# Attention, a dense FFN and a routed top-1 FFN on one core: the routing's comparisons made ahead, the last pass's tiles turned together, the last item's turns in other banks

## The chip, the cores and the metric

The kernel runs on one core of one Trainium2 chip. The metric is the device time of one execution in microseconds (us); lower is better. TensorE does the matmuls and transposes, VectorE (DVE), ScalarE (ACT) and GpSimd (POOL) the elementwise work, and DMA queues issued by SyncE (SP) and GpSimd move the data.

## What is computed

```python
x = softmax(rot(q) @ rot(k).T / 8) @ v        # 2 batches, 8 heads, 576 tokens, 64 wide -> 1152 x 512
h = x @ w_in                                  # 512 -> 2048
x = (h * sigmoid(1.702 * h)) @ w_out          # 2048 -> 512
logits = x @ w_gate                           # 8 experts
e = argmax(logits); gate = softmax(logits)[e]
out[i] = gate[i] * (relu(x[i] @ w1[e]) @ w2[e])   # 512 -> 1024 -> 512
```

A token counts only if fewer than 288 tokens before it chose the same expert; otherwise its row stays zero. So each token needs its rank among the tokens of its expert. Data and weights are float32.

## The kernel before

Weights and activations are split into a high and a low half (`hl`, `gh`, `gl`), and each product is three matmuls. ScalarE makes the high half and VectorE the low one (`halves` L833 and L834; `relu` L899 and L900). The splits of the weights live in a ring of four; the raw weights come through the buffers `wf`.

Attention goes first, in eight pairs of heads. Then the dense FFN runs in three passes over the tokens, at columns `CUTS` 0, 512, 768 and 1152. `first(k0, k1)` does a pass: `ffn` (first product `h` L853, second product `y` L883), then the finished rows `row` (L927) of 128 tokens each, which go to DRAM as `x2`, and their logits. The first two passes get the logits by eight dot products of a row on VectorE (L945). The last pass does it tile after tile on TensorE: four transposes into a bank `tr` (L936), a copy `yt` (L938), four matmuls with the gate weights into `lt` (L941) and a copy to `logits` (L942).

When all logits of a batch are known, `route(b)` runs: 25 comparisons of 128 x 128 on VectorE (L974, `before`: does a token stand ahead of another in the order that counts), 25 small matmuls that turn them into ranks (`rank` L1010), many small VectorE steps, and `r_at` (L1047), the place of each token in the list of its expert. Five scatters by GpSimd (`slots` L1059) write the list. `gather` reads it back (`ent` L1131) and fetches the tokens' rows of `x2` by indirect DMA (`got` L1136). `turn` transposes these (`tg` L1154) and splits them (`xt` L1162, L1163).

The routed FFN then works on items: `STATIC = (3, 96), (2, 112), (3, 96), (1, 96)`, that is blocks and tokens of a block; items 0 and 1 are of batch 0, items 2 and 3 of batch 1. Items 0 to 2 go through `second`: weights by `slice_of`, the products by `ffn`, the result to `yt`, transposed back, scaled by the gate (`row`) and scattered to `out` (L1183, GpSimd). `turn(i + 1)` is called from a hook of item i. Item 3, 96 tokens, goes through `few`, where the tokens stand in the partitions and the inner activations are transposed in a bank `tf` (L1251) that belongs to the same pool (`ps_m`) as all other transposes. It is a generator: its first product is issued in item 2's end. Its last row is scaled in two halves, by ScalarE (L1284) and VectorE (L1285). A loop behind it, for tokens beyond the four items, isn't entered.

Each engine does its instructions in order. The order isn't written out in this part: a scheduler chooses it from the program's order, the dependences and its estimate of times, so a change in one place can move instructions in others.

Of the kernel before, what the change touches and what calls it, by code (L numbers as in the profile page):

```python
# [25 lines left out]
P = 128  # L26
# [191 lines left out]
def consts():  # L218

    half = D // 2  # L220
    inv_freq = 1.0 / 10000.0 ** (np.arange(0, half, dtype=np.float32) / half)
    freqs = np.outer(np.arange(S, dtype=np.float32), inv_freq)
    cos, sin = np.cos(freqs), np.sin(freqs)
    main, rest = places()
    place = np.concatenate([rest, main, rest, rest])
    d = np.arange(P) % D
    cs, sn = (x[place][:, d % half].T for x in (cos, sin))
    sn = np.where((d < half)[:, None], -sn, sn)
    turns = np.stack([cs, sn], axis=1)
# [12 lines left out]
    c = np.clip(np.arange(-OFF, NC * P), 0, S - 1)  # L242
    order = np.concatenate([
        np.repeat((c // HALF * HALF + col[c % HALF])[None], P, 0),
        place.reshape(P, -1),
        valid.reshape(P, -1),
        (FAR * (1 - valid)).reshape(P, -1),
    ], axis=1)
# [9 lines left out]
    return {  # L258
        "turns": turns,
        "ident": ident,  # L260
        "rows": rows,
        "pad": pad,
        "order": order.astype(np.float32),
        "small": np.repeat(small.astype(np.float32)[None], P, 0),
    }
# [452 lines left out]
class Experts:  # L718


    def __init__(self, ctx, tc, d, cst, xt, weights):
# [6 lines left out]
        self.made, self.open, self.dots = {}, {}, []  # L728
# [32 lines left out]
    def prepare(self):  # L761
# [17 lines left out]
        self.order = one.tile([P, OFF + NC * P + 3 * B * NC], F32, name="order")  # L779
# [19 lines left out]
    def setup(self):  # L799
# [6 lines left out]
        load(self.order, d["order"])  # L806
        load(self.small, d["small"])
# [51 lines left out]
    def ffn(self, x, slices, act, hook=None, rows=False):  # L859
# [8 lines left out]
        for f in range(n + LAG):  # L868
            while len(hls) < min(n, f + 2):
                hls.append(slices[len(hls)]())  # L870
            if hook and f == n - hook[0]:
                hook[1]()
# [31 lines left out]
    def first(self, k0, k1, hook=None):  # L904
# [13 lines left out]
        y = self.ffn(self.xt[:, :, :, k0:k1], slices, self.gated, hook, rows=True)  # L918
# [6 lines left out]
        for k, t in zip(range(k0 // P, k1 // P), y):  # L925
            row = self.three.tile([P, DM], F32, name="row")
            nc.scalar.activation(out=row, in_=t, func=AF.Copy)  # L927
# [4 lines left out]
            out = [self.logits[b][:, k - b * (NC - 1)] for b in range(B) if 0 <= k - b * (NC - 1) < NC]  # L932
            if last:
                t = self.ps_m.tile([P, 512], F32, tag="m", name="tr")
                for j in range(ND):
                    nc.tensor.transpose(t[:, j * P:(j + 1) * P], row[:, j * P:(j + 1) * P], self.cst["ident"])  # L936
                yt = self.two.tile([P, ND, HALF], F32, name="yt", bufs=1)[:, :, 0:P]
                nc.vector.tensor_copy(out=yt, in_=t.rearrange("p (j c) -> p j c", j=ND))  # L938
                t = self.ps_m.tile([P, 512], F32, tag="m", name="lt")[:, 0:E]
                for j in range(ND):  # L940
                    nc.tensor.matmul(t, yt[:, j], self.gate[:, j], start=j == 0, stop=j == ND - 1)  # L941
                nc.vector.tensor_copy(out=out[0], in_=t)  # L942
                continue
            for e in range(E):
                nc.vector.scalar_tensor_tensor(  # L945
# [7 lines left out]
                )  # L953
            for x in out[1:]:
                nc.vector.tensor_copy(out=x, in_=out[0])

    def route(self, b, L):
# [34 lines left out]
        at = OFF + NC * P  # L992
        place, valid, away = (self.order[:, at + (B * i + b) * NC:at + (B * i + b + 1) * NC] for i in range(3))
        sequence = self.order[:, OFF * (1 - b):OFF * (1 - b) + NC * P]
# [13 lines left out]
        for i in range(NC):  # L1008
            for k in range(NC):
                nc.tensor.matmul(  # L1010
                    rank[:, i], before[i][:, k], oh[:, k], start=k == 0, stop=k == NC - 1
                )
# [34 lines left out]
        placed = v.tensor_copy(out=at, in_=lin)  # L1047
        ls, ex, sm, gate = big("ls"), big("ex"), col("sm"), col("gate")
# [146 lines left out]
    def second(self, ent, x, expert, hook=None, ahead=None):  # L1195
# [4 lines left out]
        y = self.ffn(x, [lambda f=f: self.slice_of(expert, f) for f in range(F2 // P)], self.relu, hook)  # L1200
# [3 lines left out]
        if ahead:  # L1204
            next(ahead)
# [10 lines left out]
    def few(self, ent, x, expert):  # L1216
# [6 lines left out]
        raws, parts = [], []  # L1223
# [24 lines left out]
        def turned(g):  # L1248
            t = self.ps_m.tile([P, 2, size], F32, tag="m", name="tf")
# [11 lines left out]
        for k in range(n + 1):  # L1261
# [38 lines left out]
    def run(self):  # L1300
# [6 lines left out]

        self.logits = [self.two.tile([P, NC, E], F32, name=f"logits{b}", bufs=1) for b in range(B)]
        for n, (k0, k1) in enumerate(zip(CUTS, CUTS[1:])):
            self.first(k0, k1, {0: (10, self.setup), len(CUTS) - 2: (0, lambda: turn(0))}.get(n))  # L1310
            if n == 0:
                self.clear()
            for b in range(B):
                if k0 < (b + 1) * S <= k1:
                    self.route(b, self.logits[b])
                    for k in range(2 * b, 2 * b + 2):
                        found[k] = self.gather(k, [b], *STATIC[k])
        def few():
            yield from self.few(found[3][0], x[3], self.expert(3, sp))

        last = few()
        for i in range(3):
            hook = (4, 0, 4)[i], lambda: turn(i + 1)
            self.second(found[i][0], x[i], self.expert(i, sp), hook, last if i == 2 else None)
        for _ in last:
            pass
# [41 lines left out]
```

## Time and profile before

| | |
|---|---|
| time, median of 3 runs | 452.94 us (452.74 to 454.37) |
| the profiled execution | 453.61 us |
| its span in the trace | 451.9 us |
| mean granted TensorE clock | 0.985 of full speed |
| PE busy | 428.3 us (95%), 3190 matmuls |
| PE weight loads (PEld) | 353.2 us (78%) |
| DVE busy | 343.3 us (76%) |
| ACT busy | 265.3 us (59%) |
| POOL busy | 134.3 us (30%) |
| DMA | 59.28 MB, mean 131 GB/s |

Times in the trace count from the span's start; 1.7 us of the execution lie outside the span. A matmul's row in a timeline may stand for several in sequence (x4), and matmuls overlap, so the step from one start to the next is shorter than one's duration. In brackets stands how long the engine was idle before an instruction and what ended that.

### The profile page before, as it was taken

How to read it: one execution, taken by the hardware profiler on the slowest of the kernel's cores; microseconds unless marked ns; L12 is line 12 of the kernel's file. 1: busy time of each engine (PE TensorE's matmuls, PEld its weight loads, DVE VectorE, ACT ScalarE, POOL GpSimd, SP SyncE). 2: the span in 40 equal slices, each digit the busy share in tenths (PEclk: the TensorE clock that was granted, in tenths of full speed). 3: DMA queues.
4: the chain of work that ended last, by engine and by line, in shares of the span. 5: the costliest groups of instructions: out<-in, count | busy, mean ns of one | idle time of the engine just before them, and what ended most of it. 6: DMA issues, size and time to landing. Idle time of an engine off the chain costs nothing.

```text
span 451.9 us, 8634 instructions
## 1 busy us (share of the span) xinstructions
PE 428.3 (95%) x3190; PEld 353.2 (78%) x3190; DVE 343.3 (76%) x815; ACT 265.3 (59%) x556; POOL 134.3 (30%) x129
## 2 busy tenths in 40 slices
PE   6799999999999999999999999999999999499994
PEld 3566666666675888888899999989889999499982
DVE  5777867788988899995599988988454899255662
ACT  1688988988786234445566665744472555163562
POOL 0988769692338000000000000003350025501011
PEclk9999999999999999999999999999999999699998
DMA  8534422612351866662133001000764346936501
GB/s 271 211 114 147 147 72 77 241 30 94 97 175 70 269 197 228 216 248 93 46 135 123 3 0 48 0 2 0 280 211 140 116 131 178 261 94 217 195 20 51
DMA packets 20542, 59.28 MB, mean 131 GB/s; under 512 B 3397, under 2 KB 5637, under 8 KB 20496
## 3 DMA queue, kind: packets, MB, share of 16 engines
q1 hardware_dynamic: 17872, 54.28, 35.9%
q0 software_dynamic: 1664, 3.62, 2.8%
q10 hardware_dynamic: 960, 0.79, 0.5%
q8 instruction: 27, 0.44, 0.4%
q14 instruction: 19, 0.16, 0.1%
HBM read 52.09 MB, written 6.67 MB: 130 GB/s over the span
## 4 chain that ended last, share of the span: by engine, by line
PE 71%; issue 13%; POOL 6%; DMA 4%; DVE 3%; ACT 1%; POOLq 0%; DVEq 0%
PE y L883 24%; PE h L853 23%; PE t L607 8%; PE s L492 6%; PE t L532 6%; PE s L753 2%; PE s L481 2%; POOL qk L465 2%; POOL out L1183 2%; DMA qk<-in_qk 1%; DMA slots<-entry,r_at 1%; DMA turns<-in_turns 1%; POOL qk L467 1%; POOL slots L1059 1%; DMA ent<-slots 1%
## 5 line engine op out<-in xcount | busy, mean ns | idle before, releaser
L853 PE MATMUL h<-xt,hl 128*128 128x256 f32 (+4 forms) x828 | 148.4, 320 | 0.0
L853 PEld LDWEIGHTS h<-xt,hl 128*128 128x128 f32 x828 | 129.8, 192 | 10.3
L834 DVE TENSOR_TENSOR hl<-wf,hl 128x1024 fp32r<-128x1024 f32 x69 | 84.6, 1226 | 23.6 <-ACT hl L833 23.3
L833 ACT ACTIVATE hl<-wf 128x1024 fp32r<-128x1024 f32 x69 | 73.1, 1061 | 40.7 <-PE y L883 21.5
L883 PE MATMUL y<-hl,gh 128*128 128x512 f32 x288 | 81.0, 392 | 0.0
L1059 POOL DMA_INDIRECT slots<-entry,r_at x10 | 13.9, 1390 | 202.6 <-DVE r_ends L970 200.2
L883 PEld LDWEIGHTS y<-hl,gh 128*128 128x128 f32 x288 | 52.9, 188 | 9.2
L504 DVE TENSOR_SCALAR_CACHE_REDUCE pp<-s 128x576 f32<-128x576 f32 x64 | 45.9, 754 | 13.6 <-PE s L492 13.0
L516 ACT ACTIVATE pp<-pp,nm 128x576 f32<-128x576 f32 x64 | 49.3, 776 | 11.3 <-DVE pp L504 11.1
L893 ACT ACTIVATE g<-h 128x256 f32<-128x256 f32 (+2 forms) x45 | 21.8, 484 | 55.6 <-PE h L853 55.5
L465 POOL TENSOR_TENSOR qk<-qk,turns 128x640 f32<-128x640 f32 (+1 forms) x30 | 44.8, 1509 | 21.3 <-DMA qk<-in_qk 21.3
L883 PE MATMUL y<-hl,gl 128*128 128x512 f32 x144 | 48.2, 392 | 0.0
L492 PE MATMUL s<-qk 64*128 64x288 f32 x256 | 40.4, 421 | 2.7 <-DVE qk L467 1.9
L607 PE MATMUL t<-pt,vr 128*64 128x288 f32 x256 | 38.0, 417 | 0.0
L532 PEld LDWEIGHTS t<-ident,pp 64*128 64x128 f32 x576 | 25.8, 138 | 13.1 <-issue 4.2
L883 PE MATMUL y<-gh,hl 128*128 128x288 f32 (+1 forms) x192 | 35.4, 297 | 0.0
L945 DVE SCALAR_TENSOR_TENSOR dot<-row,dots 128x512 f32<-128x512 f32 x48 | 33.0, 687 | 1.6 <-ACT row L927 1.2
L895 DVE TENSOR_TENSOR gl<-g,gh 128x512 fp32r<-128x512 f32 (+2 forms) x48 | 26.7, 562 | 9.6 <-ACT gh L894 9.6
L413 ACT ACTIVATE pt<-t 128x512 f32<-128x512 f32 (+1 forms) x55 | 28.5, 543 | 7.8 <-PE t L532 7.6
L532 PE MATMUL t<-ident,pp 64*128 64x64 f32 x576 | 29.8, 229 | 1.6 <-ACT ptr L413 1.1
L492 PEld LDWEIGHTS s<-qk 64*128 64x128 f32 x256 | 24.1, 188 | 7.5 <-DVE qk L467 2.8
L883 PEld LDWEIGHTS y<-hl,gl 128*128 128x128 f32 x144 | 26.2, 188 | 4.2
(185 smaller groups left out, 608.4 us busy)
## 6 DMA issues: line engine op xcount, KB each, us to landing
wf<-in_w SPq DMA_DIRECT2D x32, 512.0 KB, 4.7
qk<-in_qk SPq DMA_DIRECT2D x14, 640.0 KB, 5.0
raw<-in_w_in SPq DMA_DIRECT2D x16, 512.0 KB, 4.0
raw<-in_w_out SPq DMA_DIRECT2D x16, 512.0 KB, 4.3
vr<-in_v SPq DMA_DIRECT2D x8, 320.0 KB, 3.9
out<-got SPq DMA_DIRECT2D x9, 256.0 KB, 3.1
dots<-in_w_dots SPq DMA_DIRECT2D x4, 512.0 KB, 4.1
x<-row SPq DMA_DIRECT2D x8, 256.0 KB, 2.4
```

Of the source, the lines that this page charges most:

```text
L413: return e.activation(out=out, in_=x, func=AF.Copy)
L465: e.tensor_tensor(out=u, in0=u, in1=self.turns[:, k, ts], op=ALU.mult)
L492: nc.tensor.matmul(both[h][:, n, 0:HALF], q[hs, at:at + P], k[hs, key:key + HALF], start=True, stop=True)
L504: self.nc.vector.tensor_scalar(out=self.room(p, i).rearrange("p (n k) -> p n k", n=2), in0=self.open.pop(("s", p, i))[:, :, 0:HALF], scala ...
L516: self.nc.scalar.activation(out=x, in_=x, func=AF.Exp, scale=-1.0, bias=self.nm[p % 2][:, i:i + 1], accum_out=self.sum[p % 2][:, i:i + 1],)
L532: self.nc.tensor.transpose(banks[b][:, at:at + 64], x[bs], self.ident[bs, bs])
L607: self.nc.tensor.matmul(o[h * 64:h * 64 + 64], x, y, start=j < 2, stop=j > 7)
L833: ins = nc.scalar.activation(out=hl[:, 0], in_=t, func=AF.Copy)
L834: self.last = nc.vector.tensor_tensor(out=hl[:, 1], in0=t, in1=hl[:, 0].bitcast(F32), op=ALU.subtract).ins
L853: ins = self.nc.tensor.matmul(h, u, v, start=m == 0, stop=m == len(ops) - 1)
L883: nc.tensor.matmul(y[j][:, 0:DM if rows else w], u, v, start=f == LAG and m == 0, stop=f == n + LAG - 1 and m == 2,)
L945: nc.vector.scalar_tensor_tensor(out=self.weights.m2.tile([P, DM], F32, tag="m", name="dot"), in0=row, scalar=1.0, in1=self.dots[e], op0=A ...
```

## The change

The comparisons of batch b leave `route(b)` and become `compare(b)`, called from hooks in the passes in front: batch 0's in the second pass, batch 1's in the last. There are five of 128 x 640 for a batch, instead of 25 of 128 x 128, and they are written into the two buffers that held raw weights. Their operand, `sequence`, is an input of its own now, loaded into the `yt` tile.

In the last pass `turned_logits` turns the three tiles into three banks (one of the second product, two of `ps_m`), with copies by VectorE, ScalarE and VectorE; the logits of all three go into one bank and are copied once. The three rows are copied by ScalarE, VectorE and ScalarE. `route` and `gather` are called by `known(k)` as soon as the logits of a batch's last tile are there. The dot products of the second pass that come behind `route(0)` are ordered behind its `r_at` (`placed`).

In the last item, `few` is no generator any more, the transposes `tf` use two banks of the second product (`y1`, `y2`), and the last row is scaled by one ScalarE instruction.

```diff
     def first(self, k0, k1, hooks, known):
...
-        for k, t in zip(range(k0 // P, k1 // P), y):
+        work = []
+        for n, (k, t) in enumerate(zip(range(k0 // P, k1 // P), y)):
             row = self.three.tile([P, DM], F32, name="row")
-            nc.scalar.activation(out=row, in_=t, func=AF.Copy)
+            if last and n % 2:
+                nc.vector.tensor_copy(out=row, in_=t)
+            else:
+                nc.scalar.activation(out=row, in_=t, func=AF.Copy)
...
-            if last:
-                t = self.ps_m.tile([P, 512], F32, tag="m", name="tr")
-                for j in range(ND):
-                    nc.tensor.transpose(t[:, j * P:(j + 1) * P], row[:, j * P:(j + 1) * P], self.cst["ident"])
-                yt = self.two.tile([P, ND, HALF], F32, name="yt", bufs=1)[:, :, 0:P]
-                nc.vector.tensor_copy(out=yt, in_=t.rearrange("p (j c) -> p j c", j=ND))
-                t = self.ps_m.tile([P, 512], F32, tag="m", name="lt")[:, 0:E]
-                for j in range(ND):
-                    nc.tensor.matmul(t, yt[:, j], self.gate[:, j], start=j == 0, stop=j == ND - 1)
-                nc.vector.tensor_copy(out=out[0], in_=t)
-                continue
+        if last:
+            self.turned_logits(work)
+            known(k1 // P - 1)
+            return
...
+                if self.placed:
+                    self.tc.add_manual_dep(ins.ins, self.placed, Weights.order, reason="order")
...
+    def turned_logits(self, work):
+        nc = self.nc
+        yt = self.two.tile([P, ND, HALF], F32, name="yt", bufs=1)
+        spare = lambda: self.ps_y[3].tile([P, 512], F32, tag="y3", name="tr")
+        rooms = [yt[:, :, 0:P], yt[:, :, P:2 * P], self.three.tile([P, DM], F32, name="got", bufs=4)]
+        rooms[2] = rooms[2].rearrange("p (j c) -> p j c", j=ND)
+        for n, (row, out) in enumerate(work):
+            t = self.ps_m.tile([P, 512], F32, tag="m", name="tr") if n else spare()
+            for j in range(ND):
+                nc.tensor.transpose(t[:, j * P:(j + 1) * P], row[:, j * P:(j + 1) * P], self.cst["ident"])
+            t = t.rearrange("p (j c) -> p j c", j=ND)
+            if n % 2:
+                nc.scalar.activation(out=rooms[n], in_=t, func=AF.Copy)
+            else:
+                nc.vector.tensor_copy(out=rooms[n], in_=t)
+        t = spare()[:, 0:len(work) * E].rearrange("p (n e) -> p n e", e=E)
+        for n, (row, out) in enumerate(work):
+            for j in range(ND):
+                nc.tensor.matmul(t[:, n], rooms[n][:, j], self.gate[:, j], start=j == 0, stop=j == ND - 1)
+        nc.vector.tensor_copy(out=self.logits[B - 1][:, NC - len(work):], in_=t)
+
+    def compare(self, b):
+        at = OFF * (1 - b)
+        rooms = [self.weights.room().rearrange("p a b -> p (a b)").bitcast(BF16) for i in range(2)]
+        self.before = [rooms[k // 3][:, k % 3 * NC * P:(k % 3 + 1) * NC * P] for k in range(NC)]
+        for k in range(NC):
+            place = self.order[:, b * NC + k:b * NC + k + 1]
+            self.nc.vector.tensor_scalar(
+                out=self.before[k], in0=self.sequence[:, at:at + NC * P], scalar1=place, scalar2=None, op0=ALU.is_gt
+            )
...
     def route(self, b, L):
...
-        before = []
-        for i in range(NC):
-            x = self.one.tile([P, NC, P], BF16, name="before", bufs=2)
-            for k in range(NC):
-                ts(x[:, k], sequence[:, i * P:(i + 1) * P], place[:, k:k + 1], ALU.is_gt)
-            before.append(x)
...
     def few(self, ent, x, expert):
...
-            t = self.ps_m.tile([P, 2, size], F32, tag="m", name="tf")
+            j = 1 + len(turns) % 2
+            t = self.ps_y[j].tile([P, 512], F32, tag=f"y{j}", name="tf")[:, 0:2 * size]
...
-            if k == 0:
-                yield
...
-        half = DM // 2
-        nc.scalar.activation(out=row[:, half:], in_=y[:, half:], func=AF.Copy, scale=gate)
-        nc.vector.tensor_scalar(out=row[:, 0:half], in0=y[:, 0:half], scalar1=gate, scalar2=None, op0=ALU.mult)
+        nc.scalar.activation(out=row, in_=y, func=AF.Copy, scale=gate)
...
+            hooks = {10: self.setup}, {8: lambda: self.compare(0)}, {8: lambda: self.compare(1), 0: lambda: turn(0)}
+            self.first(k0, k1, hooks[n], known)
```

**The order on VectorE, in the routing of batch 1.** `r_...` are the routing's small steps, `hl` and `gl` the splits for item 0. Before:

```order
L1005 CAST r_s_3855<-r_s_3854 128x8
L834 TENSOR_TENSOR hl_74<-wf,hl_74 128x1024
L900 SCALAR_TENSOR_TENSOR gl<-h,gh 128x288
L974 TENSOR_SCALAR before<-order 128x128 x10
L980 SCALAR_TENSOR_TENSOR r_kc<-r_left,count 128x8
L834 TENSOR_TENSOR hl_75<-wf,hl_75 128x1024
L974 TENSOR_SCALAR r_items<-r_kc 128x8
L980 SCALAR_TENSOR_TENSOR r_key<-r_kc,small 128x8
L900 SCALAR_TENSOR_TENSOR gl<-h,gh 128x288
L974 TENSOR_SCALAR before<-order 128x128 x5
L980 SCALAR_TENSOR_TENSOR r_items<-r_kc,r_items 128x8
```

With the change:

```order
L1032 CAST r_s_3802<-r_s_3801 128x8
L903 SCALAR_TENSOR_TENSOR gl<-h,gh 128x288
L837 TENSOR_TENSOR hl_74<-wf,hl_74 128x1024
L1005 TENSOR_TENSOR r_far<-rank,r_left 128x40
L1015 SCALAR_TENSOR_TENSOR r_kc<-r_left,count 128x8
L1015 SCALAR_TENSOR_TENSOR r_far<-r_far,rank 128x40
L1009 TENSOR_SCALAR r_items<-r_kc 128x8
L1015 SCALAR_TENSOR_TENSOR r_key<-r_kc,small 128x8
L1015 SCALAR_TENSOR_TENSOR r_items<-r_kc,r_items 128x8
L1005 TENSOR_TENSOR r_sq<-r_key 128x64
L1012 TENSOR_REDUCE r_ni<-r_items 128x1
L903 SCALAR_TENSOR_TENSOR gl<-h,gh 128x288
```

The comparisons are gone from here, and the ranks are read (`r_far`) right behind the first split. Counted on to `r_at`, five `gl` of item 0 stand ahead of it now, eight before.

**The order on TensorE, from the last pass's end into item 0.** `tr` are the transposes of the rows; with L979 `tr` is the bank of the logits, L941 (`lt`) before. Before:

```order
L1154 MATMUL tg<-ident,got 128x96 x4
L936 MATMUL tr<-ident,row 128x128 x4
L941 MATMUL lt<-gate,yt 128x8 x4
L853 MATMUL h<-xt,hl_74 128x288 x2
L936 MATMUL tr<-ident,row 128x128 x4
L853 MATMUL h<-xt,hl_74 128x288 x22
L941 MATMUL lt<-gate,yt 128x8 x4
L936 MATMUL tr<-ident,row 128x128 x4
```

With the change:

```order
L1182 MATMUL tg<-ident,got 128x96 x4
L970 MATMUL tr<-ident,row 128x128 x8
L979 MATMUL tr<-gate,yt 128x8 x4
L856 MATMUL h<-xt,hl_74 128x288 x2
L970 MATMUL tr<-ident,row 128x128 x4
L979 MATMUL tr<-gate,yt 128x8 x4
L856 MATMUL h<-xt,hl_74 128x288 x19
L979 MATMUL tr<-gate,got 128x8 x4
```

All twelve transposes and eight of the twelve logits matmuls stand ahead of the long run of `h`; before, eight and four. Further on, the 25 `rank` matmuls of batch 1 stand in one block, 36 `h` and `y` matmuls behind the last row shown; before, ten stood together and 15 in ten pieces among item 0's matmuls.

**The order on GpSimd, from batch 1's scatters on.** Before:

```order
L1059 DMA slots<-entry_3936,r_at 5760x4 x5
L1131 DMA ent<-slots 96x3x4
L1131 DMA ent<-slots 96x4
L1183 DMA out<-row,ent 1152x512 x2
L1136 DMA got<-x_1867,ent 96x512 x4
L1183 DMA out<-row,ent 1152x512 x7
```

With the change:

```order
L1087 DMA slots<-entry_3883,r_at 5760x4 x5
L1159 DMA ent<-slots 96x3x4
L1159 DMA ent<-slots 96x4
L1164 DMA got<-x_1867,ent 96x512 x4
L1211 DMA out<-row,ent 1152x512 x9
```

The two `out` that stood ahead of the `got` of items 2 and 3 stand behind them now.

## Rows read from the trace of the kernel before

**Rows 1.** Window of the three passes: length, PE, PEld, DVE, ACT, POOL busy, PEclk, DMA, GB/s

```profile
160.00:337.00 177.00, 177.00 (x940) 155.10 (x939) 146.93 (x336) 94.64 (x145) 14.38 (x12) 1.00 0.32 109
```

**Rows 2.** Waits of PE: what for, us in total, times, longest

```profile
PE tg L1154 <- DMA got<-x,ent: 6.4, 1, 6.4
...
PE lt L941 <- DVE yt L938: 0.8, 1, 0.8
...
PE y L1271 <- ACT gh L1254: 0.4, 1, 0.4
...
PE y L1271 <- DVE gl L1255: 0.4, 1, 0.4
```

**Rows 3.** Windows behind the long wait, columns as in rows 1

```profile
390.00:392.00 2.00, 0.71 (x5) 0.74 (x5) 0.00 (x0) 0.00 (x0) 1.60 (x2) 0.50 1.03 258
392.00:394.00 2.00, 2.00 (x12) 2.00 (x11) 0.56 (x1) 0.49 (x1) 0.00 (x0) 0.50 0.96 207
394.00:396.00 2.00, 2.00 (x11) 2.00 (x11) 0.39 (x1) 0.36 (x1) 0.00 (x0) 0.50 0.20 76
396.00:398.00 2.00, 2.00 (x16) 2.00 (x15) 0.00 (x0) 0.04 (x1) 0.00 (x0) 0.74 0.00 0
```

**Rows 4.** Timeline of DVE, routing of batch 1: start us, us, what, [idle before, releaser]

```profile
350.04 0.17 DVE L942 COPY logits<-lt 128x8 f32<-128x8 f32 x1 [1.08 <-PE lt L941]
...
353.79 0.20 DVE L970 TENSOR_TENSOR r_oh<-r_sc,order 128x40 bf16<-128x40 f32 x1
...
355.91 0.46 DVE L900 SCALAR_TENSOR_TENSOR gl<-h,gh 128x288 fp32r<-128x288 f32 x1 [0.28 <-ACT gh L899]
356.29 2.04 DVE L974 TENSOR_SCALAR before<-order 128x128 bf16<-128x128 f32 x10
...
367.93 0.45 DVE L900 SCALAR_TENSOR_TENSOR gl<-h,gh 128x288 fp32r<-128x288 f32 x1
...
368.49 0.17 DVE L1047 CAST r_at<-r_lin 128x5 int32<-128x5 f32 x1
```

**Rows 5.** Timeline of POOL, batch 1's scatters and gathers, columns as in rows 4

```profile
368.95 1.05 POOL L1059 DMA_INDIRECT slots<-entry,r_at  x1 [34.49 <-DVE r_ends L970]
...
380.89 1.31 POOL L1131 DMA_DIRECT2D ent<-slots  x2 [3.79 <-DMA slots<-entry,r_at]
382.50 1.38 POOL L1183 DMA_INDIRECT out<-row,ent  x1 [0.30 <-issue]
384.18 1.23 POOL L1183 DMA_INDIRECT out<-row,ent  x1 [0.30 <-DMA ent<-slots]
385.71 1.01 POOL L1136 DMA_INDIRECT got<-x,ent  x1 [0.30 <-issue]
```

**Rows 6.** The chain that ended last, from 348 to 400: start us, us, what

```profile
380.89 3.38 DMA ent<-slots
```

**Rows 7.** Timeline of PE, item 0 and the start of item 2, columns as in rows 4

```profile
349.05 0.95 PE L941 MATMUL lt<-gate,yt 128*128 128x8 f32 x8
...
359.01 0.29 PE L883 MATMUL y<-gl,hl 128*128 128x288 f32 x1
...
359.21 0.38 PE L883 MATMUL y<-gh,hl 128*128 128x288 f32 x1
...
391.29 0.87 PE L1154 MATMUL tg<-ident,got 96*128 96x96 f32 x4 [6.39 <-DMA got<-x,ent]
```

**Rows 8.** Groups by line, a row's copy: busy us, mean ns, idle before

```profile
L927 ACT ACTIVATE row<-y 128x512 f32<-128x512 f32 x9 | 4.9, 595 | 0.6 <-PE y L883 0.6
```

**Rows 9.** Timeline at the end of the span, columns as in rows 4

```profile
445.51 0.47 ACT L1284 ACTIVATE row<-y,ent 96x256 f32<-96x256 f32 x1 [1.99 <-PE y L1271]
446.02 0.48 DVE L1285 TENSOR_SCALAR row<-y,ent 96x256 f32<-96x256 f32 x1 [1.83 <-ACT row L1284]
```

**Rows 10.** DMA issues from 355 to 400: KB each, median us to landing

```profile
got<-x,ent POOLq DMA_INDIRECT x4, 5.9
```

**Rows 11.** Tile `got` over the run

```profile
DMA to landing us min/median/max: 2.3/3.7/7.2
```

More of the change, by code (lines that the diff above doesn't have):

```diff
@@ L778, in prepare @@
         self.rows = one.tile([P, B, NC, 4], I32, name="rows")
-        self.order = one.tile([P, OFF + NC * P + 3 * B * NC], F32, name="order")
+        self.order = one.tile([P, 3 * B * NC], F32, name="order")
         self.small = one.tile([P, NC * E + 2 * ROWS * E + ROWS], F32, name="small")
@@ L806, in setup @@
         load(self.order, d["order"])
+        yt = self.two.tile([P, ND, HALF], F32, name="yt", bufs=1).rearrange("p a b -> p (a b)")
+        self.sequence = yt[:, 0:OFF + NC * P]
+        load(self.sequence, d["sequence"])
         load(self.small, d["small"])
@@ L857, in hidden, with ffn @@
         return gh, gl
-    def ffn(self, x, slices, act, hook=None, rows=False):
+    def ffn(self, x, slices, act, hooks, rows=False):
         nc = self.nc
@@ L870, in ffn @@
                 hls.append(slices[len(hls)]())
-            if hook and f == n - hook[0]:
-                hook[1]()
+            if n - f in hooks:
+                hooks[n - f]()
             if len(gs) <= f < n:
@@ L902, in relu, with first @@
         )
-    def first(self, k0, k1, hook=None):
+    def first(self, k0, k1, hooks, known):
         nc = self.nc
@@ L931, in first @@
                     nc.sync.dma_start(out=self.x2[b][lo - b * S:hi - b * S, :], in_=row[lo - k * P:hi - k * P])
[L932 to L943 removed]
+            work.append((row, [self.logits[b][:, k - b * (NC - 1)] for b in range(B) if 0 <= k - b * (NC - 1) < NC]))
+        if last:
+            self.turned_logits(work)
+            known(k1 // P - 1)
+            return
+        for k, (row, out) in zip(range(k0 // P, k1 // P), work):
             for e in range(E):
[L945 removed]
+                ins = nc.vector.scalar_tensor_tensor(
                     out=self.weights.m2.tile([P, DM], F32, tag="m", name="dot"),
@@ L991, in route @@
         red(fm, sc, ALU.max)
[L992 to L1000 removed]
+        valid, away = (self.order[:, (B * i + b) * NC:(B * i + b + 1) * NC] for i in (1, 2))
         oh, s0, s16 = new("oh", NC, E, dt=BF16), new("s0", E), new("s16", E, dt=BF16)
@@ L1010, in route @@
                 nc.tensor.matmul(
-                    rank[:, i], before[i][:, k], oh[:, k], start=k == 0, stop=k == NC - 1
+                    rank[:, i], self.before[k][:, i * P:(i + 1) * P], oh[:, k], start=k == 0, stop=k == NC - 1
                 )
@@ L1193, in send, with second @@
         self.sent.append(ins)
-    def second(self, ent, x, expert, hook=None, ahead=None):
+    def second(self, ent, x, expert, hook=None):
         nc = self.nc
@@ L1199, in second @@
         w = blocks * size
-        y = self.ffn(x, [lambda f=f: self.slice_of(expert, f) for f in range(F2 // P)], self.relu, hook)
+        y = self.ffn(x, [lambda f=f: self.slice_of(expert, f) for f in range(F2 // P)], self.relu, {hook[0]: hook[1]} if hook else {})
         yt = self.two.tile([P, ND, HALF], F32, name="yt", bufs=1)
@@ L1222, in few @@
         assert self.cuts % RING == 0 and RING == 4
-        raws, parts = [], []
+        raws, parts, turns = [], [], []
         def cut(k, part):
@@ L1306, in turn, with known @@
             x[i] = self.turn(found[i][1], i, None if i else self.newest)
+        def known(k):
+            b = k // (NC - 1) - 1
+            if k % (NC - 1) or b < 0:
+                return
+            self.route(b, self.logits[b])
+            for i in range(2 * b, 2 * b + 2):
+                found[i] = self.gather(i, [b], *STATIC[i])
         self.logits = [self.two.tile([P, NC, E], F32, name=f"logits{b}", bufs=1) for b in range(B)]
         for n, (k0, k1) in enumerate(zip(CUTS, CUTS[1:])):
-            self.first(k0, k1, {0: (10, self.setup), len(CUTS) - 2: (0, lambda: turn(0))}.get(n))
+            hooks = {10: self.setup}, {8: lambda: self.compare(0)}, {8: lambda: self.compare(1), 0: lambda: turn(0)}
+            self.first(k0, k1, hooks[n], known)
             if n == 0:
                 self.clear()
[L1313 to L1321, printed above, removed]
         for i in range(3):
[L1323 to L1326, printed above, removed]
+            self.second(found[i][0], x[i], self.expert(i, sp), ((4, 0, 4)[i], lambda: turn(i + 1)))
+        self.few(found[3][0], x[3], self.expert(3, sp))
         n = nc.values_load(self.etab[0:1, ITEMS:ITEMS + 1], min_val=4, max_val=ITEMS)
```

12 lines of the change are left out of this document (7 added, 5 removed).

## The prediction

> **What bounds the kernel now.** I first read the windows of the stretch that the change touches. From 160 to 337 us TensorE is busy in 177.00 of 177 us, while VectorE is busy in 146.93 and ScalarE in 94.64 [rows 1]. So there the time is TensorE's instruction stream: work taken from VectorE or ScalarE gains nothing unless TensorE stood waiting for it. The question for each edit is therefore which wait of TensorE it ends, or which matmul time it removes.
>
> The second view is TensorE's list of waits. The longest by far is 6.39 us at `tg` (L1154), the first transpose of item 2's tokens, which waits for the gathered tile `got`; there is 0.8 us at `lt` for the copy `yt`, and twice 0.4 us at L1271 for `gh` and `gl` of the last item [rows 2]. The third view, the windows behind the long wait, says what it costs besides. TensorE had been idle for 6.39 us, and the granted clock reads 0.50, the lower level (1.2 GHz of 2.4), from 390 to 396 us, 0.74 in the next two and after that it is back [rows 3]. Work lost: 0.71 us busy at half speed is 0.36, 392 to 396 is 4 x 0.5 = 2.0, and 396 to 398 is 2 x 0.26 = 0.52; together **2.87 us**. The wait and its clock cost 9.26 us.
>
> Fourth, what the tile waits for, by the timelines of VectorE and GpSimd and the chain of waits. Batch 1's logits are known at 350.04, but `r_at`, the places that the scatters need, is cast only at 368.49 [rows 4]. The five scatters begin at 368.95, `ent` is issued at 380.89 and lands 3.38 us later at 384.27, two scatters `out` of earlier rows take the queue at 382.50 and 384.18, and only at 385.71 is the first `got` issued [rows 5, 6]; TensorE starts on the tile at 391.29 [rows 7]. From `r_at` to `tg` that is 22.8 us of small steps, and `r_at` itself is 18.4 us behind its logits.
>
> **The change, part by part.** *The late gather.* The 18.4 us are not the routing's own work. VectorE does its queue in order, and between the logits and `r_at` stand splits `hl` and `gl` for the expert, each held by ScalarE and TensorE. In the order before, the eighth `gl` of item 0 (367.93) stands ahead of `r_at`, and the comparisons stand in two groups, ten in 2.04 us from 356.29 and five behind [rows 4], with the matmuls that rank tokens between them. In the order of the change the comparisons are gone from here, the 25 rank matmuls stand in one block, and `r_at` stands behind the fifth `gl` of item 0. The fifth `gl` started at 355.91 and took 0.46 us [rows 4], so `r_at` comes at about 356.5, **12 us earlier**. GpSimd's queue is also reordered: four `got` now stand ahead of all nine `out`, so the 1.44 us from the landing of `ent` (384.27) to the first `got` (385.71) go too [rows 5, 6]. The tile is ready at about 391.29 - 12 - 1.4 = 377.9. TensorE was there at 391.29 - 6.39 = 384.90 and will come some 1.9 us sooner by the next two terms, at 383.0. Five us of slack remain, so the wait ends, and with it the idle stretch ahead of the fall of the clock: **-6.39 - 2.87 = -9.26**. What is late next is nothing near: the item's weights are loaded as their buffers come free, as before.
>
> *Three tiles turned at once.* Before, each tile's transposes, copy, matmuls and copy ran one behind the other in one bank, with the wait of 0.8 at the first `lt` [rows 2] and the last one's matmuls (0.95 us for eight at 349.05 [rows 7]) among item 0's. Now 12 transposes and two of three groups of matmuls stand ahead of item 0's main run, in time in which TensorE waited anyway. Taken from the flow: the matmuls at 349.05 and a later group of transposes; against that the third row's copy now waits for all three accumulations at the end of the pass. The nearest row for a row's copy is 595 ns [rows 8]. I take a gain of **1.0**, between a loss of 0.5 (one copy more on the path) and a gain of 2.0 (the 0.95, the 0.8 and a smaller wait).
>
> *Rank matmuls in one block.* In the order before, the last 15 of the 25 stand in ten pieces among item 0's matmuls, and a `y` behind such a piece lasted 0.38 against 0.29 for one among its kind [rows 7]: 10 x 0.09 = **0.9**. The block's matmuls themselves are the same 25.
>
> *Comparisons.* Fifty small ones for two batches become ten of 128 x 640. Their price isn't in the trace; ten small ones took 2.04 us, 0.204 each [rows 4], so a wide one lies between 0.2 (all fixed cost) and 5 x 0.204 = 1.02 (all per element), five between 1 and 5 us. I need neither: batch 0's run at the end of the first pass and batch 1's in the second half of the routing of batch 0, under VectorE's 30 us of idle time in the window of 177 [rows 1]. If that cover were gone at a split, 5 us of one batch would be the cost; none is booked.
>
> *The end.* The last row was scaled by halves, ScalarE 0.47 from 445.51 and VectorE 0.48 from 446.02 to 446.50: 0.99 us, one behind the other [rows 9]. One ScalarE instruction over 512 columns is bounded by 0.47 and the 595 ns of a row's copy over as many columns [rows 8]; I take the latter: 0.99 - 0.6 = **0.39**. The last item's turns get two other banks instead of sharing those of the transposes; the two waits at L1271 [rows 2] sum to 0.8, of which I take **0.4**, between nothing better (and 0.5 lost, since the last item's first product no longer runs ahead at item 2's end) and all 0.8.
>
> **Sum.** 9.26 + 1.0 + 0.9 + 0.39 + 0.4 = 11.95. The profiled execution took 453.61 us, 0.67 above the median of the runs, 452.94. So 441.7 by the one and 441.0 by the other; I say **441.5**. The four small terms, 2.7 in sum, could be 0.3 to 4.2 by their ends (the scaling at most 0.99 - 0.47 = 0.52), so this case lies between 439.5 and 444.
>
> **Rivals.** *1: the transfers set the tile.* The gathers of item 2 now issue at about 372 to 377, amid other weight loads. In 355 to 400 a gather landed 5.9 us after its issue (median), against 2.3, 3.7 and 7.2 (least, median, most) over the run [rows 10, 11]. If each trip behind `r_at` (scatters, `ent`, `got`) is stretched so that the tile comes 9.5 us later than in my sum, at 387.4, TensorE waits 4.3 us and loses a share of the clock, 2.87 x 4.3 / 6.39 = 1.9: 447.7; with half of that delay or less, the slack takes it. For it: the long trips were in the very stretch where the weights flow. Against it: the five us of slack, and that the trip of 5.9 is in my sum already. Middle 445.5. The Trainium skill, "DMA: Bandwidth & Descriptors", section "Queues, rings and completion order", says that an SDMA engine takes turns between the queue rows that it has work for, a whole packet from each; by that rule a gather beside weight loads waits for their packets in turn. The trace agrees as far as it goes, 5.9 against 3.7 us, but shows no gather here without loads.
>
> *2: the order doesn't bring the 12 us.* `r_at` stands behind work that other engines release; if the fifth `gl` and the splits ahead of it come later, so that `r_at` is only 5 us earlier, the tile is ready at 384.9 and TensorE waits 1.8 us plus 0.8 of clock: 444.1. Against it: five `gl` need no more than item 0's own progress, which is TensorE's.
>
> *3: slower.* TensorE takes its queue in order, so the block of 25 rank matmuls holds everything behind it until VectorE has `r_oh`, and each us late is a us of TensorE. Before, `r_oh` came 3.9 us after the logits (350.04 to 353.79 and its 0.20) [rows 4]; now some 36 matmuls of about 0.13 us, 4.7 us, stand between the last logits matmul and the block. So the stall is nothing or a us; a slower kernel than before by the bound below needs 11.95 + 2.3 = 14 us of stall (455.3). Only a split that waits for a weight load ahead of `r_oh` on VectorE could do that.
>
> **How the numbers follow.** Forecast 0.80, rival 1 0.12, rival 2 0.05, rival 3 0.03. The range goes a little below the forecast's own end, to 439.0 (all the small gains, on the median's basis), and up to 446.5, which takes in rival 2 and most of rival 1. A measurement of this kernel tells about 0.5%, 2.3 us, from no change: faster by more than that in the forecast, rival 2 and nearly all of rival 1, 0.93; within it 0.04, from a worse rival 1; slower 0.03.
>
> **What would show it.** Right: no wait of TensorE at `tg` of item 2 and a granted clock of 1.00 from 375 to 390; `r_at` about 12 us earlier; four `got` directly behind the two `ent` on GpSimd; at most one group of `lt`-like matmuls still among item 0's first products; one scaling of 0.6 us at the end. Wrong: a wait at the rank block, a wait at `tg` that has only moved, or a new wait of a split for weights; a total above 447 would mean that the long wait is still there.

## The result: 441.0 us, and the profile after

The changed kernel takes 441.0 us, the median of four runs (440.29 to 441.54), against 453.04 of the kernel before beside it. The ratio is 0.9728, with a 95% interval of 0.9704 to 0.9752: 2.7% faster, 12.0 us by the medians. The forecast was 441.5 in a range of 439.0 to 446.5. The profiled execution took 440.29 us, 13.3 less than the one of before.

The page of the changed kernel:

```profile
span 438.6 us, 8587 instructions
PE 424.1 (97%) x3190; PEld 350.2 (80%) x3190; DVE 337.5 (77%) x772; ACT 265.1 (60%) x556; POOL 135.0 (31%) x129
```

TensorE issues as many matmuls as before, in 13.3 us less. Its list of waits, longest first:

```profile
PE s L492 <- DVE qk L467: 1.9, 2, 1.0
PE t L446 <- DVE warm L429: 1.3, 1, 1.3
```

All that is left lies in the attention. The 6.4 us at `tg`, the 0.8 at `lt` and the two of 0.4 at the last item's `y` [rows 2] are gone. VectorE in the routing of batch 1:

```profile
344.77 0.18 DVE L980 COPY logits<-tr 128x24 f32<-128x24 f32 x1 [0.95 <-PE tr L979]
...
347.60 0.20 DVE L1005 TENSOR_TENSOR r_oh<-r_sc,order 128x40 bf16<-128x40 f32 x1
...
356.17 0.45 DVE L903 SCALAR_TENSOR_TENSOR gl<-h,gh 128x288 fp32r<-128x288 f32 x1
...
356.93 0.17 DVE L1074 CAST r_at<-r_lin 128x5 int32<-128x5 f32 x1
```

`r_at` comes behind the fifth `gl`, at 356.93 instead of 368.49 [rows 4]; 356.5 was forecast. The logits come at 344.77 instead of 350.04; counted from the last `tg` ahead of them (336.85, before 337.42) that is 4.7 us earlier, and `r_at` 11.0. GpSimd behind it:

```profile
357.38 1.01 POOL L1087 DMA_INDIRECT slots<-entry,r_at  x1 [23.34 <-DVE r_ends L1005]
...
368.49 1.29 POOL L1159 DMA_DIRECT2D ent<-slots  x2 [4.04 <-DMA slots<-entry,r_at]
371.65 1.03 POOL L1164 DMA_INDIRECT got<-x,ent  x1 [1.87 <-PE h L856]
...
377.08 1.21 POOL L1211 DMA_INDIRECT out<-row,ent  x1 [0.30 <-issue]
```

The first `got` is issued at 371.65, 14.1 us earlier than in [rows 5], and no `out` stands ahead of it. TensorE:

```profile
336.85 0.49 PE L1182 MATMUL tg<-ident,got 96*128 96x96 f32 x4
...
349.42 0.78 PE L1037 MATMUL rank<-r_oh,raw 128*128 128x8 bf16 x25
...
382.29 0.49 PE L1182 MATMUL tg<-ident,got 96*128 96x96 f32 x4
...
395.16 1.04 PE L1236 MATMUL tr<-ident,yt 128*112 128x128 f32 x8
...
432.15 0.39 PE L1300 MATMUL y<-hl,gl 128*96 128x512 f32 x1
```

`tg` of item 2 at 382.29 has no idle time ahead of it, and the window there shows the full clock and TensorE busy throughout (length, PE, PEld, DVE, ACT, POOL, PEclk, DMA, GB/s):

```profile
380.00:390.00 10.00, 10.00 (x94) 10.00 (x94) 6.54 (x10) 5.61 (x10) 1.35 (x1) 1.00 0.69 243
```

The same three marks in the trace before (the last `tg` ahead of the turned tiles, the transposes of item 1's last rows, the last `y`):

```profile
337.42 0.49 PE L1154 MATMUL tg<-ident,got 96*128 96x96 f32 x4
...
406.93 1.04 PE L1210 MATMUL tr<-ident,yt 128*112 128x128 f32 x8
...
445.09 0.39 PE L1271 MATMUL y<-hl,gl 128*96 128x512 f32 x1
```

From the first mark to the second it was 69.51 us and is 58.31: **11.20 gained**. The forecast's 9.26 for the wait and its clock leaves 1.94 for the rest. The start of item 2's `tg` divides the 11.20 without an estimate. Before, TensorE was free for `tg` 47.48 us after the first mark (391.29 less the wait of 6.39), and now it starts it at 45.44: 2.04. The wait is 6.39. From the start of `tg` to the second mark 15.64 became 12.87: 2.77 for the clock. From the second mark to the third 38.16 became 36.99: **1.17**. From the last `y` to the end of the span 6.81 became 6.45: **0.36**. The other 0.57 lies ahead of the first mark. There the traces below, but for that of the last item alone, scatter from 335.85 to 338.66, so it can't be told from noise.

In two of the experiments below one execution was slow, at a lower granted clock (450.46 us of the comparisons alone, 460.29 of the last item alone, the one with the trace); the ratios leave these two out, the medians take them in.

### The profile page after: what moved, and what is told of

It is laid out like the page before. It is cut to its first block, busy times and chain, and to the rows that moved or that the text cites. A ratio compares the mean times of both kernels' runs of the same rounds, so it can differ in the third digit from the quotient of the medians.

```text
span 438.6 us, 8587 instructions
## 1 busy us (share of the span) xinstructions
PE 424.1 (97%) x3190; PEld 350.2 (80%) x3190; DVE 337.5 (77%) x772; ACT 265.1 (60%) x556; POOL 135.0 (31%) x129
## 4 chain that ended last, share of the span: by engine, by line
PE 76%; issue 12%; POOL 5%; DVE 3%; DMA 2%; ACT 1%; POOLq 0%; DVEq 0%
PE y L886 26%; PE h L856 25%; PE t L607 8%; PE s L492 6%; PE t L532 6%; PE s L753 2%; PE s L481 2%; POOL out L1211 2%; POOL qk L465 2%; DMA qk<-in_qk 1%; DMA turns<-in_turns 1%; POOL qk L467 1%; PE tr L979 1%; DVE pp L504 1%; DVE gl L898 0%
## 5 line engine op out<-in xcount | busy, mean ns | idle before, releaser
L856 PEld LDWEIGHTS h<-xt,hl 128*128 128x128 f32 x828 | 128.3, 189 | 10.5
L886 PE MATMUL y<-hl,gh 128*128 128x512 f32 x288 | 82.7, 391 | 0.0
L886 PE MATMUL y<-hl,gl 128*128 128x512 f32 x144 | 50.0, 392 | 0.0
L886 PE MATMUL y<-gh,hl 128*128 128x288 f32 (+1 forms) x192 | 32.8, 288 | 0.0
```

Of the source, the lines that this page charges most:

```text
L856: ins = self.nc.tensor.matmul(h, u, v, start=m == 0, stop=m == len(ops) - 1)
L886: nc.tensor.matmul(y[j][:, 0:DM if rows else w], u, v, start=f == LAG and m == 0, stop=f == n + LAG - 1 and m == 2,)
```

## The experiments

The times are medians; the ratio is to the kernel before, run beside them on the same chip, whose median was 452.6 to 454.2 each time.

| kernel | us (lowest to highest) | ratio, 95% interval |
|---|---|---|
| comparisons alone | 446.86 (443.16 to 450.46) | 0.9849 (0.9763 to 0.9936) |
| turned tiles alone | 447.46 (444.16 to 448.48) | 0.9873 (0.9811 to 0.9935) |
| last item alone | 451.65 (450.03 to 460.29) | 0.9970 (0.9942 to 0.9997) |
| change without the last item's part | 442.73 (441.98 to 444.12) | 0.9783 (0.9739 to 0.9827) |
| change, list read once more | 439.71 (439.53 to 443.63) | 0.9727 (0.9662 to 0.9791) |
| change, list read twice more | 443.14 (440.96 to 444.07) | 0.9781 (0.9733 to 0.9830) |
| before, comparisons into the raw buffers | 443.52 (443.20 to 447.67) | 0.9813 (0.9747 to 0.9880) |
| change, comparisons called in the routing | 439.82 (439.47 to 441.14) | 0.9698 (0.9652 to 0.9745) |
| change with small comparisons in the routing | 441.30 (440.29 to 444.25) | 0.9758 (0.9698 to 0.9818) |
| change, `tf` in the common pool | 440.68, one run | |
| change, last row in halves | 441.28, one run | |

### The parts one by one

**The comparisons alone** (the kernel before with `compare`, its hooks, `sequence` and the raw buffers):

```diff
-                    rank[:, i], before[i][:, k], oh[:, k], start=k == 0, stop=k == NC - 1
+                    rank[:, i], self.before[k][:, i * P:(i + 1) * P], oh[:, k], start=k == 0, stop=k == NC - 1
...
+            hooks = {10: self.setup}, {8: lambda: self.compare(0)}, {8: lambda: self.compare(1), 0: lambda: turn(0)}
+            self.first(k0, k1, hooks[n])
```

> The kernel before with the comparisons moved to the passes in front and nothing else of the change. In its order seven `gl` of item 0 stand ahead of `r_at` (eight before, five with the whole change), and the four `got` stand ahead of the `out`. Theory (the time of `r_at` follows the `gl` it stands behind, and that sets the wait): the seventh `gl` started at 364.19 before, so `r_at` at about 364.7, 3.8 us earlier, 1.4 more by GpSimd's order; the rank block saves 0.9 of TensorE. So the wait at item 2's `tg` falls from 6.4 to some 1 to 2 us, with under 1 us of clock: 443.5 to 446.5. Rival (any one part frees enough, since the change left five us of slack): no wait, 442 to 443. Rival (the comparisons are off the path): the wait stays at 5 to 6 us, 451 to 453.

Its VectorE timeline and TensorE's marks:

```profile
364.95 0.46 DVE L903 SCALAR_TENSOR_TENSOR gl<-h,gh 128x288 fp32r<-128x288 f32 x1 [0.22 <-ACT gh L902]
365.32 0.16 DVE L1052 CAST r_at<-r_lin 128x5 int32<-128x5 f32 x1
```

```profile
338.66 0.49 PE L1159 MATMUL tg<-ident,got 96*128 96x96 f32 x4
...
385.09 0.52 PE L1159 MATMUL tg<-ident,got 96*128 96x96 f32 x4
...
397.99 1.04 PE L1215 MATMUL tr<-ident,yt 128*112 128x128 f32 x8
```

`r_at` follows the seventh `gl`. In this execution (444.97 us) the tile came in time, with no wait. The median of all four, 446.86, lies a little above what was expected; that of the three in the ratio is 444.97, inside the range. These three spread from 443.16 to 448.75, the four of the change over 1.3 us. A gather without slack would do that, but only one execution has a trace, so it is not shown. From first to second mark it is 59.33 us; without the wait and its clock before had 69.51 - 9.26 = 60.25. So the rank matmuls in one block are worth **0.92** by the forecast's price of the clock. Up to the start of `tg`, which needs no such price, it is 46.43 against 47.48: **1.05**. TensorE's waits ahead of `tg` are the same in both traces, so this is matmul time: in that stretch the 25 rank matmuls are busy for 0.78 us in one block and for 2.33 in pieces, part of it overlapped by others.

**The turned tiles alone** (`turned_logits`, the row copies by ScalarE, VectorE and ScalarE; comparisons as before):

```diff
+        if last:
+            self.turned_logits(work)
+            return
```

> The kernel before with the last pass's three tiles turned together and nothing else of the change; the 25 comparisons of a batch stay in the routing. Seven `gl` stand ahead of `r_at`, the `got` ahead of the `out`. Theory: as for the comparisons alone, `r_at` 3.8 us earlier and 1.4 by GpSimd's order, 1.0 of TensorE at the end of the pass: a wait of 1 to 2 us, 443.5 to 446.5. Rival (any one part frees enough): no wait, 442 to 443. Rival (logits that come earlier help nothing while 15 comparisons stand behind them): wait 5 to 6 us, 451 to 453.

```profile
336.39 0.49 PE L1172 MATMUL tg<-ident,got 96*128 96x96 f32 x4
...
385.19 0.52 PE L1172 MATMUL tg<-ident,got 96*128 96x96 f32 x4 [2.32 <-DMA got<-x,ent]
...
399.72 1.04 PE L1228 MATMUL tr<-ident,yt 128*112 128x128 f32 x8
```

```profile
385.20:386.00 0.80, 0.80 (x8) 0.80 (x9) 0.02 (x1) 0.25 (x1) 0.80 (x1) 1.00 0.97 369
386.00:387.00 1.00, 1.00 (x9) 1.00 (x8) 0.56 (x1) 0.24 (x1) 0.70 (x2) 0.72 1.06 283
387.00:388.00 1.00, 1.00 (x7) 1.00 (x7) 0.39 (x1) 0.36 (x1) 0.69 (x2) 0.50 1.10 246
388.00:389.00 1.00, 1.00 (x6) 1.00 (x6) 0.00 (x0) 0.00 (x0) 0.70 (x2) 0.50 0.93 279
389.00:390.00 1.00, 1.00 (x8) 1.00 (x7) 0.00 (x0) 0.00 (x0) 0.80 (x1) 0.57 1.10 291
```

The wait is 2.3 us, and the granted clock falls to its lower level only when TensorE is at work again. It costs 0.28 + 0.50 + 0.50 + 0.43 = 1.7 us; from `tg` to the second mark it is 14.53 against the 12.87 of the change, 1.66 more. The median, 447.46, is 1.0 us above the range expected, in which I had put the clock at under a us; the traced execution took 446.45. TensorE is free for `tg` 46.48 us after the first mark, 1.00 sooner than before. Before, it waited 0.78 us for `yt` and 0.39 at `tr` at the end of the last pass; here these are gone, and one of 0.19 for a row's copy has come. That is the 1.0.

So the turned tiles alone don't free enough, and logits that come earlier do help behind 15 comparisons: both of its rivals fall. For the comparisons alone the trace shows no wait, and whether they free enough in every execution stays open. Counted from the first mark, `r_at` is as early in the one (26.66) as in the other (26.79), but from `r_at` to the first `got` it took 15.8 us with the comparisons alone, 17.1 with the turned tiles alone and 14.7 with the change.

**The last item alone**, and **the change without it**:

```diff
-        half = DM // 2
-        nc.scalar.activation(out=row[:, half:], in_=y[:, half:], func=AF.Copy, scale=gate)
-        nc.vector.tensor_scalar(out=row[:, 0:half], in0=y[:, 0:half], scalar1=gate, scalar2=None, op0=ALU.mult)
+        nc.scalar.activation(out=row, in_=y, func=AF.Copy, scale=gate)
```

(with `tf` in `y1` and `y2`, and `few` no generator; the second kernel turns these three back.)

> The kernel before with the last item's part alone: `tf` in the banks of `y1` and `y2`, no generator, one scaling of the last row. Theory: the wait of 6.4 us at item 2's `tg` is as before; at the end 0.3 to 0.4 us less by the scaling and 0.4 to 1.2 less of waits at L1271: 451.5 to 452.4. Rival (the end's gain in the trace of the change came of the granted clock or of the earlier gather): within 0.3 us of before.

> The changed kernel with the last item as before (generator, `tf` in the common pool, scaling by halves). Theory: the order up to item 2 is that of the change, no wait at item 2's `tg`; the end costs 0.8 to 1.5 us more than the change: 441.8 to 442.5. Rival (the last item's part is worth nothing): 440.8 to 441.3.

As the theory had it: the first takes 1.0 us less than before (451.65 against 452.64), the second 442.73, 0.2 above its range. Its ratio of 0.9783 lies above the 0.9728 of the change, but the intervals overlap, so the traces have to tell. In the trace of the change without the last item's part the two waits are back, and from the second mark to the last `y` it is 38.18 us, as before; in that of the last item alone it is 36.99, as in the change. So the gain at the end comes neither of the earlier gather nor of the clock.

```profile
395.63 1.04 PE L1238 MATMUL tr<-ident,yt 128*112 128x128 f32 x8
...
433.81 0.39 PE L1299 MATMUL y<-hl,gl 128*96 128x512 f32 x1
```

```profile
PE y L1299 <- ACT gh L1282: 0.4, 1, 0.4
...
PE y L1299 <- DVE gl L1283: 0.4, 1, 0.4
```

### How much room the gather has now

```diff
         nc.gpsimd.dma_start(out=ent, in_=src)
+        if isinstance(item, int) and item == 2:
+            for _ in range(1):
+                nc.gpsimd.dma_start(out=ent, in_=src)
```

(`range(2)` in the second one.)

> The changed kernel with the list `ent` of item 2 read once more before the gathers are issued, so that they come later by one landing: about 2.4 us and 0.3 of issue, 3 us in all; the order on TensorE stays that of the change. Theory (the tile now has about five us to spare): no wait at item 2's `tg`, 440.5 to 441.5. Rival (there is no room left, the wait was only just removed): a wait of about 3 us and a share of clock, 444 to 446.

> The changed kernel with the list read twice more: the gathers come some 5.5 to 7 us later. Theory (five us to spare): a wait of 0.5 to 2 us, and if it is near 2 us another 1.7 of clock, as in the run of the turned tiles alone where 2.3 us of waiting were followed by 3.5 us at the lower granted clock: 441.5 to 445. Rival (every us of delay costs a us and its clock from the start): 447 to 450. Rival (TensorE finds other work): 441.

Once more costs nothing (0.9727, the ratio of the change): the first `got` is issued at 374.40, with the time of the first mark taken off 3.4 us later than in the change, and TensorE doesn't wait in the trace. One of its four executions took 443.63 us, and why isn't known. Its first mark and its first `got`:

```profile
336.23 0.50 PE L1185 MATMUL tg<-ident,got 96*128 96x96 f32 x4
```

```profile
374.40 1.02 POOL L1167 DMA_INDIRECT got<-x,ent  x1 [2.77 <-DMA ent<-slots]
```

Twice more is near the edge. Of that kernel GpSimd and TensorE:

```profile
378.31 1.03 POOL L1167 DMA_INDIRECT got<-x,ent  x1 [3.38 <-PE tr L1239]
```

```profile
337.44 0.49 PE L1185 MATMUL tg<-ident,got 96*128 96x96 f32 x4
...
382.88 0.49 PE L1185 MATMUL tg<-ident,got 96*128 96x96 f32 x4
```

Here the gather is 6.1 us later than in the change, and in this execution (440.96 us, the fastest of the four) the tile still came in time. The median is 3.4 us above that of the kernel with one more read. So 3.4 us of delay cost nothing by the medians, and about 6 do; the forecast's five us of room lie between. That the other three executions wait at `tg` is not shown: no trace of one was kept, and their mean granted clock (0.994 to 0.996) is not below that of the traced one (0.992).

### Why the comparisons came earlier: the place of the calls, or the room

In the kernel before, `before` was a ring of two tiles for five groups of comparisons, and its trace has VectorE wait twice, 1.0 us in sum, for `rank` ahead of them:

```profile
DVE before L974 <- PE rank L1010: 1.0, 2, 0.8
```

The next kernel is the one before with only this:

```diff
         before = []
+        rooms = [self.weights.room().rearrange("p a b -> p (a b)").bitcast(BF16) for i in range(2)]
         for i in range(NC):
-            x = self.one.tile([P, NC, P], BF16, name="before", bufs=2)
+            x = rooms[i // 3][:, i % 3 * NC * P:(i % 3 + 1) * NC * P].rearrange("p (n c) -> p n c", n=NC)
```

> The kernel before with one thing changed: the 25 small comparisons of a batch, still called in the routing, are written to the two buffers of the raw weights, where all five groups have room, instead of a ring of two. Theory B (the ring of two held them back, since the third group waits for rank matmuls; the calls in the passes in front and the wide form matter little): the scheduler puts them ahead of the routing by itself, seven `gl` ahead of `r_at`, the rank matmuls in one block, so it runs as the comparisons alone did: 443 to 449, a wait between 0 and 3 us. Rival (the 50 small instructions cost more of VectorE than ten wide ones, 10.2 us against 5.5, and this reaches TensorE): 2 us or more slower than the comparisons alone.

```profile
362.90 0.16 DVE L1048 CAST r_at<-r_lin 128x5 int32<-128x5 f32 x1
```

```profile
382.92 0.52 PE L1155 MATMUL tg<-ident,got 96*128 96x96 f32 x4 [0.19 <-DMA got<-x,ent]
```

It gives 0.9813, as much as the comparisons alone in all their parts (0.9849, the intervals overlap), with a wait of 0.19 us. The other two turn it round in the changed kernel: the same wide comparisons called in the routing, with `sequence` in a tile of its own (that part of the diff is left out here),

```diff
-            hooks = {10: self.setup}, {8: lambda: self.compare(0)}, {8: lambda: self.compare(1), 0: lambda: turn(0)}
+            hooks = {10: self.setup}, {}, {0: lambda: turn(0)}
...
+        self.compare(b)
         valid, away = (self.order[:, (B * i + b) * NC:(B * i + b + 1) * NC] for i in (1, 2))
```

> The changed kernel with `compare(b)` called in the routing, not from the hooks in the passes in front; five wide comparisons in the raw weights' buffers as in the change, and `sequence` in a tile of its own. Theory B (room, not the place of the call): the scheduler moves them ahead all the same, five `gl` ahead of `r_at`: 440.3 to 441.6, no wait at `tg`. Rival (the hooks are what puts them ahead): `r_at` 2 us or more later, 443 to 447.

and 25 small ones called in the routing, into the raw buffers (the two diffs above put together, `sequence` in its own tile too, with no `compare` at all):

> The changed kernel without its comparisons' part but for the room: 25 small comparisons of a batch, called in the routing, no hooks, written to the raw weights' buffers; the turned tiles and the last item's part are those of the change. Theory B (room, not the calls and not the wide form): five `gl` ahead of `r_at`, no wait at item 2's `tg`, the time of the change within the noise, 439.5 to 441.5. Rival (the wide form counts, since 50 small ones take 5 us more of VectorE): 442 or more.

Neither can be told from the change: 0.9698 and 0.9758 against 0.9728, `r_at` at 357.80 and 355.82 (from the first mark 20.1 and 20.0 us, in the change 20.1), no wait at `tg`. In this order:

```profile
357.80 0.17 DVE L1074 CAST r_at<-r_lin 128x5 int32<-128x5 f32 x1
```

```profile
355.82 0.17 DVE L1071 CAST r_at<-r_lin 128x5 int32<-128x5 f32 x1
```

The hooks and the wide form aren't what helps. With room for all five groups the scheduler itself puts the comparisons of batch 1 far ahead of its routing, before 304 us in all three kernels; the wide form only takes less of VectorE's time (ten of 548 ns in the change, fifty of 280 in the last kernel). The room was that of the raw weights' buffers each time; a longer ring of their own was not run.

```profile
L988 DVE TENSOR_SCALAR raw<-yt,order x10: 546/548/554, 196.6 to 293.9; 128x640 bf16<-128x640 f32 x10
```

```profile
L998 DVE TENSOR_SCALAR raw<-sequence,order 128x128 bf16<-128x128 f32 x50 | 10.4, 280 | 0.0
```

### The end, piece by piece

The changed kernel with `tf` in `ps_m` again:

```diff
-            j = 1 + len(turns) % 2
-            t = self.ps_y[j].tile([P, 512], F32, tag=f"y{j}", name="tf")[:, 0:2 * size]
...
+            t = self.ps_m.tile([P, 2, size], F32, tag="m", name="tf")
```

> The changed kernel with `tf` in the common pool again; no generator, one scaling. Measured from the transposes of item 1's last rows to the start of the last `y`, which took 38.2 us before and 37.0 with the change. Theory (the two waits of 0.4 us at the last item's `y` come of the shared pool): both waits are back, 37.8 or more. Rival (the generator's place made them): 37.0 and no such wait.

From the second mark to the last `y` it is 395.01 to 432.61, 37.60 us: between the two theories. One of the two waits is back:

```profile
395.01 1.04 PE L1236 MATMUL tr<-ident,yt 128*112 128x128 f32 x8
...
432.61 0.40 PE L1297 MATMUL y<-hl,gl 128*96 128x512 f32 x1
```

```profile
PE y L1297 <- ACT gh L1280: 0.4, 1, 0.4
```

So the banks are worth 37.60 - 36.99 = 0.6. The rest of the 1.17 is the step from here to the change without the last item's part, 38.18 - 37.60 = 0.6, and in this stretch these two kernels differ only in the generator: it comes of issuing the last item in the program's order. Each figure is from one trace; three others with the end of the change (the last row in halves, the comparisons called in the routing, the small ones there) have 36.96 to 36.98.

The changed kernel with the last row in halves again, the diff of the last item turned back:

> The changed kernel with the last row scaled in two halves as before. Theory: from the start of ScalarE's half to the end of VectorE's 0.95 to 1.0 us, against 0.68 of the one instruction, 0.3 us more; in the whole time not to be told from noise.

```profile
432.94 0.47 ACT L1311 ACTIVATE row<-y,ent 96x256 f32<-96x256 f32 x1 [2.16 <-PE y L1300]
433.45 0.48 DVE L1312 TENSOR_SCALAR row<-y,ent 96x256 f32<-96x256 f32 x1 [1.76 <-ACT row L1311]
```

From 432.94 to 433.93 is 0.99 us, and in the change it is one instruction:

```profile
432.57 0.68 ACT L1310 ACTIVATE row<-y,ent 96x512 f32<-96x512 f32 x1 [2.15 <-PE y L1300]
```

That is 0.31 us. The halves go one behind the other although they are on two engines: VectorE's begins 0.04 us after ScalarE's end, in this trace and in [rows 9]. Both read the same bank of PSUM. The Trainium skill, "PSUM — Partial Sum Buffer", section "PSUM bank collisions raise a hardware error", says that two engines may not access one bank within the same partitions at the same time, reads included, and that the hardware doesn't arbitrate. By that the two reads have to be kept in order, and splitting a bank between two engines gains nothing. The trace agrees with the order, at 0.04 us between them; no run here lets them go together, and none separates the shared bank from the shared tile `row` as the reason.

## Why the prediction was right

- **The wait at `tg` and its clock, 9.26.** As forecast: 6.39 and 2.77, 9.16. `r_at` came 11.6 us earlier in the span, 11.0 from the first mark (12 forecast), the `out` left the way, the wait is gone and the clock stays at 1.00. The step rested on the place of `r_at` behind the fifth `gl`, and both parts are needed for that: each alone brings only the seventh, with a wait of 0 and 2.3 us in their traces.
- **What brought it.** The forecast told this as the comparisons' leaving VectorE's queue. That is half of it: the logits come 4.7 us earlier by the turned tiles. Counted from the first mark, the comparisons alone bring `r_at` 4.4 us earlier (26.66 against 31.07), the turned tiles alone 4.3 (26.79), and both 11.0, more than the sum. And the comparisons leave because they have room, not because they are called elsewhere.
- **The rank block, 0.9:** 0.92 with the forecast's price of the clock, 1.05 without it. **The turned tiles, 1.0:** from the first mark to the second 59.33 with the comparisons alone and 58.31 with both, 1.02. The forecast took it from matmuls leaving the flow and the wait at `lt`; by the traces it is the waits, 0.78 and 0.39 less 0.19.
- **The comparisons, nothing:** 548 ns each, between the bounds of 0.2 and 1.02, and TensorE waits for none.
- **The last item, 0.4:** mis-sized. It is 1.17, beyond its bounds of -0.5 and 0.8, of which 0.6 are the banks and 0.6 the place of the last item, which I had down as a possible loss of 0.5.
- **The scaling, 0.39:** 0.31; the 595 ns of a row's copy without a scale were too little for the instruction that also scales, which took 0.68 us.
- **The sum:** 9.26 + 0.92 + 1.02 + 1.17 + 0.31 = 12.7 against 11.95. The medians, 12.0 apart, can't tell the two, so that the forecast came within half a us of the median is in part luck.
- **Rival 1, the transfers,** didn't come: behind `r_at` the first `got` was issued within 14.7 us and the tile came in time. That a gather later than the slack costs time is what the median of the list read twice more suggests. Its price was too low: I had charged the clock in proportion to the wait, 2.87 x 4.3 / 6.39, and the run with 2.3 us of wait lost 1.7 by the clock instead of 1.0.
- **Rival 2,** `r_at` a few us earlier only, is what each part alone does: a wait of 2.3 us and 1.7 of clock with the turned tiles alone, where the rival had 1.8 and 0.8.
- **Rival 3, a stall at the rank block:** none. `r_oh` is there at 347.80, the block begins at 349.42.

## What to carry to other kernels

Look in the order for what a late result stands behind on an engine that goes in order: here it counted how many of another stage's splits were ahead, and each one less was worth some 4 us. Where a scheduler places the work, a ring of buffers that is too short can pin it to a late place, and room may do more than moving a call. Don't stop at the edge: the two partial versions remove most of the wait, but leave the tile little or no room to be late. Whether room also takes the scatter out of the times isn't shown: the four runs of the change lie within 1.3 us, but those with one more read of the list, or with small comparisons in the routing, spread over 4.

## What was not expected of the hardware

A short idle stretch cost more of the clock, for its length, than a long one, in one trace of each. After 6.39 us of idleness the granted clock was at the lower level for about 6 us [rows 3], 2.87 us of work; after 2.32 us it was there for about 3 (0.72, 0.50, 0.50 and 0.57 in four windows of 1 us), 1.7 us of work; after 0.19 us, with the comparisons into the raw buffers, it stayed at 1.00. In the second case it fell only when TensorE had been at work again for at least 0.8 us, so the slow matmuls stand behind the wait and look as if they belonged to the next stage.
